# Building on-chip token lists: compares on VectorE unit by unit instead of in blocks on GpSimd

## The chip, the cores and the metric

The kernel runs on one core of one Trainium2 chip. The core has five engines that run their own instruction streams in order and wait for one another through semaphores: TensorE (PE in the profile; its weight loads are PEld), VectorE (DVE), ScalarE (ACT), GpSimd (POOL) and SyncE (SP), which here only issues transfers. The metric is the device time of one execution in microseconds (us); lower is better.

## The reference, cut to what matters

The reference is a gated linear-attention layer followed by a two-level mixture of experts. Only the part that the change touches is the routing: for each of 3072 tokens a group and an expert are chosen by the largest logit, and the token is sent through that expert with a weight.

```python
g_idx = np.argmax(x @ w_group, axis=1)            # 4 groups; g_w = softmax value of the winner
e_idx = np.argmax(xg @ w_expert[g], axis=1)       # 4 experts in each group; e_w likewise
...
h = np.maximum(xg[mask_e] @ w1[g, e], 0.0)
ye = h @ w2[g, e]
out[tok_idx] = (g_w * e_w)[:, None] * ye
```

`x` is the output of the attention, B=4 batches, 8 heads, 768 steps, 40 values a head. On the chip each expert fetches its tokens by a list of row numbers, so a list of tokens (and of weights) for each of the 16 experts must be made before an expert starts.

## The kernel before, in words

**Attention.** The sequence is cut into NCH=6 chunks of 128 steps; a chunk of one batch is a *unit*, 24 units (u = 0 to 23, u = 4 * chunk + batch). `unit(u)` writes the code of one step of a software pipeline: loads for unit u+3, decays for u+2, scores of u, and the end (`norm`, `rows`, `turn`) of unit u-1. On TensorE one step is, in order, the scores (`sp`, line 192), the product with the carried state (`it`, L218), logits of an earlier unit (`lg`, L333), the state update (`st`, L238), the values (`av`, L266) and the transposes of the finished rows (`tp`, L314). VectorE has, among others, the masked scores (`pt`, L198), the sum of carried and new part (`num`, L275), the denominators (`den`, L284 to L293), the finished rows (`x`, L301) and the state addition (`Cflat`, L256). GpSimd has four instructions in each step: the causal mask (`ab`, L154, for unit u+2), the weighted keys (`kw`, L205, for u+1), the decay of the state (`Cflat`, L245, for u) and the output gate times the inverse denominator (`sr`, L295, for u-1). VectorE's `x` needs `sr`; GpSimd's decay needs TensorE's `it`.

**Routing.** When the four logits of a chunk are there, `logits` starts a generator `route(c, ...)`, a *chore*. `go_on()` stands at five places of a step and advances the first chore by one stage (up to the next `yield`), so that routing is woven into the attention. The stages find the winners (`oh`), count ranks by small matmuls (L373 to L382), and give each token a slot number (`slots`, L405), from which `lo` (slot modulo 128) and `d` (the rest) follow. The chunk's share of the lists is a matmul: for each unit b of the chunk, `marks` (L424: a 128x128 0/1 table, an iota compared with `lo`), `eh` (L428: 128x48, a constant compared with `d`) and `put` (L433: `eh` times three columns of `vals`, 128x144 for a unit, two units in one instruction); then four matmuls (L443, written to the PSUM bank named `lg`) and an addition into `lists` (L446, L448). Which engine makes them is set by `q`: GpSimd for chunks 0 to 3 and for the first three units of chunk 4, VectorE for the last unit of chunk 4 and for chunk 5.

**Order.** Steps 2 to 21 (`MANUAL` = 22) are issued exactly as written. From step 22 on a scheduler orders the instructions. After chunk 2 is routed, the chore `first_experts` picks the first two experts and the loads of their weights follow on SyncE's queue, one piece (`w1s` or `w2s`) a step (`early_loads`, from step 15 in the order before). The first expert runs on the tokens of chunks 0 to 4 (fetch `xe`, L582); a second pass adds those of chunk 5.

The change and the prediction touch `route` (L406 to L448), the end of `unit` (L850 to L860), the loop over the steps (L964 to L969), and no code of the experts. The engine is picked by one line before:

```python
q = nc.gpsimd if c < NCH - 2 or (c < NCH - 1 and n > 1) else nc.vector
```

Of the kernel before, what the change touches and what calls it, by code (L numbers as in the profile page):

```python
# [57 lines left out]
def lstm_moe(ctx: ExitStack, tc: tile.TileContext, gates, qkT, nat, og, wcat, w1, w2, cst, tab, out):  # L58
# [281 lines left out]
    def route(c, b0, b1, bank):  # L340
# [74 lines left out]
        nc.vector.tensor_copy(lo, loi)
# [3 lines left out]
        q.tensor_tensor(d, slf, lo, op=ALU.subtract)
        marks = post.tile([P, n, P], F32R, name="marks", bufs=1)  # L420
        for b in range(n):
            if b == 2:
                yield
            q.tensor_scalar(marks[:, b], iota, lo[:, b:b + 1], None, op0=ALU.is_equal)  # L424
        yield
        eh = post.tile([P, n, NEH], F32, name="eh", bufs=1)
        for b in range(n):
            q.tensor_scalar(eh[:, b], ehc, d[:, b:b + 1], None, op0=ALU.is_equal)  # L428
        put = post.tile([P, n, 3, NEH], F32R, name="put", bufs=1)
        for b in range(0, n, 2):  # L430
            yield
            m = min(2, n - b)
            rt["last"] = q.tensor_tensor(put[:, b:b + m], bc(eh[:, b:b + m].unsqueeze(2), (P, m, 3, NEH)),  # L433
                            bc(vals.bitcast(F32)[:, us][:, b:b + m].unsqueeze(3), (P, m, 3, NEH)), op=ALU.mult)
        yield
# [4 lines left out]
        yield  # L440
        lp = rt["bank"][:, B * 36 + NE:B * 36 + NE + NLIST]
        for b in range(n):
            mm(lp, marks[:, b, :], put[:, b].rearrange("p i k -> p (i k)"), start=(b == 0), stop=(b == n - 1))  # L443
        yield
        if c + b0:
            nc.vector.tensor_tensor(lists, lists, lp, op=ALU.add)  # L446
        else:
            nc.vector.tensor_copy(lists, lp)  # L448
# [713 lines left out]
```

## Time and profile before

| what | value |
|---|---|
| three runs | 469.69, 473.66, 473.73 us (median 473.66) |
| the profiled execution, own time | 474.44 us |
| its span from the first to the last instruction | 472.9 us |
| busy in the span | TensorE 425.8, VectorE 332.8, ScalarE 268.5, GpSimd 195.9 us |
| mean granted TensorE clock | 0.955 of full speed |
| step 4 starts its scores | 42.13 us |
| steps 8, 12, 16, 20 | 67.60, 98.59, 135.08, 163.37 us |
| steps 21, 22 | 174.40, 179.95 us |
| first matmul of the first expert | 206.15 us |
| experts from there to the end | 266.8 us (472.9 - 206.15) |

Rows of the trace begin with start and length in us, then the engine, the line, the operation and its operands (result <- inputs); x4 is the number of instructions merged into the row (TensorE rows count a float32 matmul's two passes, so eight matmuls stand as x16). What stands in square brackets is the time for which the engine sat idle before it and the instruction it waited for. A row of stretches gives the stretch, its length, the busy time and number of instructions of each engine, the granted TensorE clock, the busy share of the transfer engines and their rate in GB/s.

### The profile page before, as it was taken

To read this page: it belongs to the slowest core of one execution; us is meant where nothing else is said; L and a number is where in the kernel's file an instruction comes from. 1 tells how busy PE (TensorE), PEld (TensorE's weight loads), DVE (VectorE), ACT (ScalarE), POOL (GpSimd) and SP (SyncE) were. 2 spreads that over 40 slices of the span, in tenths; PEclk is the share of its full clock that TensorE was granted. 3 is DMA by queue.
4 is the path that set the end of the run, shared out by engine and by line. 5 is a ranking of instruction groups with operands and counts; after the bars stand their busy time and mean duration, and the time that the engine had idled before them with its cause. 6 is when DMAs were issued, how large, how long until landed. Compare 5 with 4: busy or idle time off the path is not lost.

```text
span 472.9 us, 9535 instructions
## 1 busy us (share of the span) xinstructions
PE 425.8 (90%) x3421; PEld 404.4 (86%) x3421; DVE 332.8 (70%) x864; ACT 268.5 (57%) x619; POOL 195.9 (41%) x233
## 2 busy tenths in 40 slices
PE   7689997989799878989999999999999999898890
PEld 5579997878698778779999999999999999797890
DVE  7545777957577757779884765867676787988850
ACT  5556756473467662172764555665657655786640
POOL 7435465592835554106524134233322553232110
PEclk9797998998899989799999999999999999999996
DMA  4997674966559950254995366486557766353000
GB/s 149 292 300 232 224 249 129 338 182 227 150 177 309 322 196 18 67 195 154 381 372 201 123 214 230 161 303 203 215 188 278 256 236 226 102 208 138 14 16 9
DMA packets 24627, 94.40 MB, mean 200 GB/s; under 512 B 3888, under 2 KB 8072, under 8 KB 20994
## 3 DMA queue, kind: packets, MB, share of 16 engines
q1 hardware_dynamic: 20178, 77.95, 48.8%
q0 software_dynamic: 4128, 15.46, 8.8%
q8 instruction: 28, 0.46, 0.4%
q10 hardware_dynamic: 272, 0.36, 0.3%
q14 instruction: 21, 0.17, 0.1%
HBM read 84.21 MB, written 10.40 MB: 200 GB/s over the span
## 4 chain that ended last, share of the span: by engine, by line
PE 59%; DVE 15%; POOL 7%; DMA 5%; issue 5%; ACT 5%; SPq 1%; POOLq 0%; ACTq 0%; DVEq 0%
PE psh L741 17%; PE sp L192 6%; PE av L266 6%; PE po L762 5%; PE po L764 5%; PE po L763 5%; PE lg L333 3%; DMA ab<-a_d 3%; DVE w2l L640 2%; PE it L218 2%; PE tpm L675 2%; POOL marks L424 2%; DVE hh L698 2%; PE po L768 1%; DVE w1l L640 1%
## 5 line engine op out<-in xcount | busy, mean ns | idle before, releaser
L586 POOL DMA_INDIRECT out_dram<-y,li x35 | 49.8, 1422 | 147.2 <-ACT y L775 107.7
L762 PE MATMUL po<-w2h,hh 128*128 128x320 f32 (+1 forms) x208 | 65.8, 316 | 0.0
L763 PE MATMUL po<-w2l,hh 128*128 128x320 f32 (+1 forms) x208 | 64.2, 309 | 0.0
L764 PE MATMUL po<-w2h,hh 128*128 128x320 f32 (+1 forms) x208 | 64.1, 308 | 0.0
L182 ACT ACTIVATE ab<-ab,bcol 128x128 f32<-128x128 f32 x184 | 56.3, 389 | 13.0 <-POOL ab L154 12.4
L640 DVE TENSOR_TENSOR w2l<-w2s,w2h 128x640 fp32r<-128x640 f32 x64 | 49.8, 817 | 16.9 <-ACT w2h L638 16.7
L741 PE MATMUL psh<-xhl,w1h 128*128 128x256 f32 (+4 forms) x352 | 58.9, 288 | 1.2 <-DVE xhl L681 1.2
L192 PE MATMUL sp<-qk 128*128 128x128 f32 x384 | 53.0, 294 | 4.8 <-DMA qk<-in_qkT_dram 4.7
L266 PE MATMUL av<-nt,pt 128*128 128x128 f32 x384 | 56.2, 305 | 0.9 <-DVE pt L198 0.9
L192 PEld LDWEIGHTS sp<-qk 128*128 128x128 f32 x384 | 49.6, 208 | 5.7 <-issue 3.3
L266 PEld LDWEIGHTS av<-nt,pt 128*128 128x128 f32 x384 | 51.2, 214 | 2.3 <-DVE pt L198 1.3
L741 PEld LDWEIGHTS psh<-xhl,w1h 128*128 128x128 f32 x352 | 49.8, 189 | 1.9 <-DVE xhl L681 1.7
L582 POOL DMA_INDIRECT xg<-x_d,li x33 | 36.9, 1119 | 30.1 <-DVE cntr L564 18.5
L640 DVE TENSOR_TENSOR w1l<-w1s,w1h 128x1024 fp32r<-128x1024 f32 x32 | 39.0, 1220 | 12.2 <-ACT w1h L638 12.2
L638 ACT CAST w2h<-w2s 128x640 fp32r<-128x640 f32 x64 | 42.9, 727 | 1.1 <-DMA w2s<-in_w_dram 1.0
L154 POOL TENSOR_SCALAR_AFFINE_SELECT ab<-ab 128x1024 f32<-128x1024 f32 (+1 forms) x25 | 26.7, 1068 | 36.4 <-DMA ab<-a_d 32.5
L695 ACT ACTIVATE hh<-psh 128x512 fp32r<-128x512 f32 (+4 forms) x56 | 28.3, 506 | 21.0 <-PE psh L741 20.7
L698 DVE SCALAR_TENSOR_TENSOR hh<-psh,hh 128x256 fp32r<-128x256 f32 (+2 forms) x84 | 33.4, 429 | 9.0 <-ACT hh L695 8.6
L762 PEld LDWEIGHTS po<-w2h,hh 128*128 128x128 f32 (+1 forms) x208 | 38.8, 187 | 0.7 <-ACT hh L695 0.2
L764 PEld LDWEIGHTS po<-w2h,hh 128*128 128x128 f32 (+1 forms) x208 | 38.8, 187 | 0.1
L763 PEld LDWEIGHTS po<-w2l,hh 128*128 128x128 f32 (+1 forms) x208 | 38.9, 187 | 0.0
L198 DVE TENSOR_TENSOR pt<-sp,ab 128x512 f32<-128x512 f32 x48 | 32.8, 685 | 8.1 <-PE sp L192 7.1
(196 smaller groups left out, 957.4 us busy)
## 6 DMA issues: line engine op xcount, KB each, us to landing
w1s<-in_w_dram SPq DMA_DIRECT2D x12, 1536.0 KB
w2s<-in_w_dram SPq DMA_DIRECT2D x12, 1280.0 KB
ab<-a_d SPq DMA_DIRECT2D x23, 512.0 KB
nt<-in_nat_dram SPq DMA_DIRECT2D x24, 324.0 KB
qk<-in_qkT_dram SPq DMA_DIRECT2D x48, 160.0 KB
x_d<-x SPq DMA_DIRECT2D x24, 192.0 KB
sig<-in_og_dram SPq DMA_DIRECT2D x6, 640.0 KB
w1s<-in_w_dram SPq DMA_DIRECT2D x4, 768.0 KB
```

The source lines that it names most:

```text
L182: rt["exp"] = nc.scalar.activation(ab[:, j, :], ab[:, j, :], AF.Exp, bias=bcol[:, c, b * H + j:b * H + j + 1])
L192: mm(sp[:, jj, :], qk[:, j % 2, j // 2, :], qk[:, 2, j // 2, :], start=True, stop=True)
L266: mm(av[:, o:o + P], t["pm"][j // 4][:, j % 4, :], nt[:, o:o + P], start=True, stop=True)
L582: return nc.gpsimd.indirect_dma_start(out=o, out_offset=None, in_=src, in_offset=bass.IndirectOffsetOnAxis(ap=idx, axis=0))
L586: return nc.gpsimd.indirect_dma_start(out=out, out_offset=bass.IndirectOffsetOnAxis(ap=idx, axis=0), in_=y, in_offset=None, bounds_check=N ...
L638: nc.scalar.copy(a, src[:, s])
L640: lows.append(lambda: nc.vector.tensor_tensor(o[rows], src[rows, s], a[rows].bitcast(F32), op=ALU.subtract))
L698: rt["dve"] = nc.vector.scalar_tensor_tensor(hh[:, f:f + per, dst], src[:, :, t], 0.0, hr.bitcast(F32)[:, :, t], op0=ALU.max, op1=ALU.subt ...
L741: ins = mm(ps[:, g * W:(g + 1) * W], w[:, s], x, start=(n == 0), stop=(n == len(todo) - 1))
L762: mm(po[0:m], hh[:, f, t], w2h[:, s], start=st0, stop=False)
L763: mm(po[0:m], hh[:, f, t], w2l[:, s], start=False, stop=False)
L764: ins = mm(po[0:m], hh[:, f, tl], w2h[:, s], start=False, stop=sp0)
```

## The change

The compares (`marks`, `eh`) of all chunks go to VectorE, and for chunks 0 to 3 they are no longer made in one block inside the chore. Each unit's pair of compares with its product `put` becomes one task in a list `heavy`; the four matmuls (`placed`) and the addition (`summed`) are two more tasks. `unit` runs one task (two from step 18 on) behind `rows`, `state2` and `values` of the step, ahead of `turn`. At step 21 what is left in the list is run at the end. GpSimd keeps only the multiplications: `d`, the weights and `put`, the latter one unit at a time. For chunks 4 and 5 (`now`) everything stays in the chore, on VectorE, with one `put` for all units, so the three units of chunk 4 move from GpSimd to VectorE too. The chore has fewer stages.

```diff
-    chores = []
+    chores, heavy = [], []
...
-        q = nc.gpsimd if c < NCH - 2 or (c < NCH - 1 and n > 1) else nc.vector
+        now = c >= NCH - 2
+        q = nc.vector if now else nc.gpsimd
+        d = post.tile([P, n], F32, name="d")
+        q.tensor_tensor(d, slf, lo, op=ALU.subtract)
...
-        for b in range(n):
-            if b == 2:
-                yield
-            q.tensor_scalar(marks[:, b], iota, lo[:, b:b + 1], None, op0=ALU.is_equal)
-        yield
-        eh = post.tile([P, n, NEH], F32, name="eh", bufs=1)
-        for b in range(n):
-            q.tensor_scalar(eh[:, b], ehc, d[:, b:b + 1], None, op0=ALU.is_equal)
-        put = post.tile([P, n, 3, NEH], F32R, name="put", bufs=1)
-        for b in range(0, n, 2):
+        def mark(b, m):
...
+            for i in range(b, b + m):
+                nc.vector.tensor_scalar(t["marks"][:, i], iota, lo[:, i:i + 1], None, op0=ALU.is_equal)
+                nc.vector.tensor_scalar(t["eh"][:, i], ehc, d[:, i:i + 1], None, op0=ALU.is_equal)
+            rt["last"] = q.tensor_tensor(t["put"][:, b:b + m].rearrange("p b (i k) -> p b i k", i=3),
...
+        def placed():
+            lp = t["lp"] = rt["bank"][:, B * 36 + NE:B * 36 + NE + NLIST]
+            for b in range(n):
+                mm(lp, t["marks"][:, b], t["put"][:, b], start=(b == 0), stop=(b == n - 1))
+
+        def summed():
+            if c + b0:
+                nc.vector.tensor_tensor(lists, lists, t["lp"], op=ALU.add)
...
+        if now:
             yield
+            mark(0, n)
+            yield
+        else:
+            heavy.extend([lambda b=b: mark(b, 1) for b in range(n)] + [placed, summed])
+            yield
...
         go_on()
+        if heavy and u < MANUAL:
+            for _ in range(2 if u > 17 else 1):
+                task = heavy.pop(0) if heavy else None
+                if task:
+                    task()
         if not late(u - 1):
             run(turn, u - 1)
...
+            if u == MANUAL - 1:
+                do(heavy)
             do(early_loads, 1 if 14 <= u < 20 else 0)
```

**Place 1: GpSimd around step 8.** Before, after the `sr` of step 7 (names as above; the first column is the code line):

```order
L295 TENSOR_TENSOR sr<-sig,den 128x320
L419 TENSOR_TENSOR d<-slots,lo 128x4
L424 TENSOR_SCALAR marks<-ks,lo 128x128 x4
L428 TENSOR_SCALAR eh<-ks,d 128x48 x4
L154 AFFINE_SELECT ab<-ab 128x1024
L433 TENSOR_TENSOR put<-eh,vals 128x288
L205 TENSOR_TENSOR kw<-nt,ab 128x320
L245 TENSOR_TENSOR Cflat<-Cflat,dec 128x328
L433 TENSOR_TENSOR put<-eh,vals 128x288
```

Now, on the same engine from the small products of step 7 on:

```order
L415 TENSOR_TENSOR d<-slots,lo 128x4
L417 TENSOR_TENSOR wf<-sm,se 128x4
L418 TENSOR_TENSOR vals<-sm,se 128x4
L419 TENSOR_TENSOR vals<-wf,vals 128x4
L295 TENSOR_TENSOR sr<-sig,den 128x320
L430 TENSOR_TENSOR put<-eh,vals 128x144
L154 AFFINE_SELECT ab<-ab 128x1024
L205 TENSOR_TENSOR kw<-nt,ab 128x320
```

Eight compares have left GpSimd; one `put` for one unit stands directly behind `sr` and ahead of the mask, in steps 7 to 10 alike. The pair of compares it waits for stands on VectorE behind `x` and the state additions:

```order
L301 TENSOR_TENSOR x<-num,sr 128x320
L256 TENSOR_TENSOR Cflat<-Cflat,st 40x4x41 x2
L428 TENSOR_SCALAR marks<-ks,lo 128x128
L429 TENSOR_SCALAR eh<-ks,d 128x48
L275 TENSOR_TENSOR num<-num,av 128x328
```

**Place 2: TensorE, the list matmuls of chunk 0.** Before, in step 8, between state update and values:

```order
L333 MATMUL lg<-wc,xT 128x20 x3
L238 MATMUL st<-nt,kw 40x41 x8
L443 MATMUL lg<-put,marks 128x144 x4
L266 MATMUL av<-nt,pt 128x128 x8
L314 MATMUL tp<-cs,x 128x128 x2
```

Now, in step 11, behind the values:

```order
L333 MATMUL lg<-wc,xT 128x20 x3
L238 MATMUL st<-nt,kw 40x41 x8
L266 MATMUL av<-nt,pt 128x128 x8
L437 MATMUL lg<-put,marks 128x144 x4
L314 MATMUL tp<-cs,x 128x128 x2
```

They move three steps later, one step behind the last `put` they need. Those of chunk 1 move from step 12 to step 17, those of chunk 2 from step 14 to step 20, those of chunk 3 from step 20 into the scheduled part behind step 21, between pieces of unit 22.

**Place 3: SyncE, the first piece of expert weights.** Before, in the issue order (`w1s` is one half of a first weight matrix, `TENSOR_LOAD ewi` reads which expert it is):

```order
L308 DMA x_d<-x 128x384 x2
L161 DMA ab<-a_d 128x1024
L139 DMA qk_93<-in_qkT_dram 40x2x512
L140 DMA qk_93<-in_qkT_dram 40x1024
L170 DMA nt<-in_nat_dram 128x648
L308 DMA x_d<-x 128x384
L592 TENSOR_LOAD ewi x2
L600 ISA
L600 DMA w1s<-in_w_dram 128x1536
```

Now:

```order
L308 DMA x_d<-x 128x384 x2
L604 TENSOR_LOAD ewi x2
L612 ISA
L612 DMA w1s<-in_w_dram 128x1536
L161 DMA ab<-a_d 128x1024
L139 DMA qk_93<-in_qkT_dram 40x2x512
L140 DMA qk_93<-in_qkT_dram 40x1024
L170 DMA nt<-in_nat_dram 128x648
L308 DMA x_d<-x 128x384
```

The first piece is issued one step earlier (at the end of step 14), and six pieces instead of five stand between the loads of the attention; the sixth stood behind the last row store before.

More of the change, by code (lines that the diff above doesn't have):

```diff
@@ L408, in route @@
         nc.vector.tensor_scalar(loi, loi, P - 1, None, op0=ALU.bitwise_and)
+        lo = post.tile([P, n], F32, name="lo")
+        nc.vector.tensor_copy(lo, loi)
         yield
-        q = nc.gpsimd if c < NCH - 2 or (c < NCH - 1 and n > 1) else nc.vector
+        now = c >= NCH - 2
+        q = nc.vector if now else nc.gpsimd
+        d = post.tile([P, n], F32, name="d")
+        q.tensor_tensor(d, slf, lo, op=ALU.subtract)
         wf = post.tile([P, n], F32, name="wf")
@@ L425, in route @@
-        yield
-        eh = post.tile([P, n, NEH], F32, name="eh", bufs=1)
-        for b in range(n):
-            q.tensor_scalar(eh[:, b], ehc, d[:, b:b + 1], None, op0=ALU.is_equal)
-        put = post.tile([P, n, 3, NEH], F32R, name="put", bufs=1)
-        for b in range(0, n, 2):
-            yield
-            m = min(2, n - b)
-            rt["last"] = q.tensor_tensor(put[:, b:b + m], bc(eh[:, b:b + m].unsqueeze(2), (P, m, 3, NEH)),
-                            bc(vals.bitcast(F32)[:, us][:, b:b + m].unsqueeze(3), (P, m, 3, NEH)), op=ALU.mult)
@@ L435, in route @@
-        yield
+        t = {}
+        def mark(b, m):
+            if not t:
+                for a, w, dt in (("marks", P, F32R), ("eh", NEH, F32), ("put", NLIST, F32R)):
+                    t[a] = post.tile([P, n, w], dt, name=a, bufs=1)
+            sh = (P, m, 3, NEH)
+            for i in range(b, b + m):
+                nc.vector.tensor_scalar(t["marks"][:, i], iota, lo[:, i:i + 1], None, op0=ALU.is_equal)
+                nc.vector.tensor_scalar(t["eh"][:, i], ehc, d[:, i:i + 1], None, op0=ALU.is_equal)
+            rt["last"] = q.tensor_tensor(t["put"][:, b:b + m].rearrange("p b (i k) -> p b i k", i=3),
+                                         bc(t["eh"][:, b:b + m].unsqueeze(2), sh),
+                                         bc(vals.bitcast(F32)[:, us][:, b:b + m].unsqueeze(3), sh), op=ALU.mult)
@@ new lines, in placed @@
+        def placed():
[6 more added lines that the diff above has]
+            else:
+                nc.vector.tensor_copy(lists, t["lp"])
+        if now:
+            yield
+            mark(0, n)
+            yield
+        else:
+            heavy.extend([lambda b=b: mark(b, 1) for b in range(n)] + [placed, summed])
+            yield
@@ L439, in route @@
         nc.vector.tensor_tensor(nxt, cur, ohs, op=ALU.add)
[L440 to L448, printed above, removed]
+        if now:
+            yield
+            placed()
+            yield
+            summed()
     def go_on(n=1):
```

5 lines of the change are left out of this document (removed).

## The prediction

> **What bounds the kernel now.** The change works in the attention, so I read first how long its steps take. The stretches below are cut at the score starts of steps 4, 8, 12, 16, 20, 21, 22 and at the first expert matmul.
>
> ```profile
> 42.13:67.60 25.47, 25.11 (x273) 24.25 (x272) 19.09 (x58) 17.22 (x52) 13.01 (x20) 1.00 0.70 226
> 67.60:98.59 30.99, 27.85 (x277) 26.28 (x276) 26.08 (x61) 17.54 (x52) 19.00 (x31) 0.94 0.71 226
> 98.59:135.08 36.49, 30.03 (x281) 28.58 (x280) 24.09 (x75) 17.54 (x52) 23.07 (x39) 0.91 0.57 172
> 135.08:163.37 28.29, 25.72 (x273) 24.51 (x272) 20.65 (x62) 20.35 (x54) 13.66 (x21) 1.00 0.92 300
> 163.37:174.40 11.03, 7.97 (x56) 7.66 (x54) 6.05 (x15) 7.05 (x14) 8.75 (x12) 0.85 0.75 268
> 174.40:179.95 5.55, 5.55 (x52) 5.48 (x52) 4.09 (x16) 4.27 (x13) 0.00 (x0) 0.99 0.01 1
> 174.40:206.15 31.75, 27.35 (x194) 24.06 (x193) 22.44 (x104) 10.06 (x31) 7.38 (x14) 0.89 0.21 69
> ```
>
> Steps 4 to 7 make no list: TensorE is busy for 25.11 of 25.47 us at full clock, and is the bound. The next four steps take 5.52 us more with four more matmuls, the four after them 11.02 more with eight; the clock falls to 0.94 and 0.91. GpSimd's busy time rises from 13.01 to 19.00 and 23.07. Steps 16 to 19 lose only 2.82, at full clock but with transfers at 0.92. So the excess sits where lists are made. The waits say which one:
>
> ```profile
> PE lg L443 <- POOL put L433: 10.2, 8, 2.9
> PE tp L314 <- DVE x L301: 6.0, 5, 2.0
> DVE x L301 <- POOL sr L295: 22.5, 13, 3.2
> ```
>
> TensorE waits 10.2 us for `put` from GpSimd, and 6.0 for `x`, which itself waits for GpSimd's `sr`. In step 8, in order of time on TensorE, GpSimd and VectorE:
>
> ```profile
> 72.37 0.44 PE L443 MATMUL lg<-put,marks 128*128 128x144 f32 x2 [0.81 <-POOL put L433]
> 74.38 0.45 PE L443 MATMUL lg<-put,marks 128*128 128x144 f32 x2 [1.57 <-POOL put L433]
> 74.67 2.87 PE L266 MATMUL av<-nt,pt 128*128 128x128 f32 x16
> 82.58 2.05 PE L266 MATMUL av<-nt,pt 128*128 128x128 f32 x16
> ```
> ```profile
> 66.51 2.63 POOL L424 TENSOR_SCALAR marks<-ks,lo 128x128 fp32r<-128x128 f32 x4
> 69.13 1.51 POOL L428 TENSOR_SCALAR eh<-ks,d 128x48 f32<-128x48 f32 x4
> 70.59 1.08 POOL L154 TENSOR_SCALAR_AFFINE_SELECT ab<-ab 128x1024 f32<-128x1024 f32 x1
> 71.65 0.66 POOL L433 TENSOR_TENSOR put<-eh,vals 128x288 fp32r<-128x288 f32 x1
> 76.03 0.72 POOL L205 TENSOR_TENSOR kw<-nt,ab 128x320 f32<-128x320 f32 x1
> ```
> ```profile
> 70.62 6.17 DVE L439 TENSOR_TENSOR ohsum<-ohsum,ohs 128x16 bf16<-128x16 bf16 x1
> ```
>
> Eight compares hold GpSimd for 4.1 us. `put` is late, TensorE stands 0.81 and 1.57 us, and the values behind it take 2.87 instead of 2.05 us, since the clock was lowered in the pause. VectorE pays too: a 16-element addition that starts at 70.62 ends at 76.79, when GpSimd's unbroken run (66.51 to 76.75) is over.
>
> **The change part by part.** Of the 16 pairs that move out of GpSimd's blocks and the three of chunk 4, VectorE's price is in the trace, where it makes those of chunk 5:
>
> ```profile
> 209.06 0.28 DVE L424 TENSOR_SCALAR marks<-ks,lo 128x128 fp32r<-128x128 f32 x1
> 209.25 0.25 DVE L428 TENSOR_SCALAR eh<-ks,d 128x48 f32<-128x48 f32 x1
> 209.41 0.48 DVE L424 TENSOR_SCALAR marks<-ks,lo 128x128 fp32r<-128x128 f32 x2
> ```
>
> Starts lie 0.19 and 0.16 us apart, so a pair costs 0.35 us. What hides it: VectorE is busy 19.09 of 25.47 us in steps 4 to 7, 1.6 us idle a step; and in the pair's own place, here step 16:
>
> ```profile
> 139.42 0.49 DVE L301 TENSOR_TENSOR x<-num,sr 128x320 f32<-128x320 f32 x1 [1.00 <-POOL sr L295]
> 139.83 0.65 DVE L256 TENSOR_TENSOR Cflat<-Cflat,st 40x164 f32<-40x164 f32 x2
> 141.06 0.49 DVE L275 TENSOR_TENSOR num<-num,av 128x328 f32<-128x328 f32 x1 [0.58 <-PE av L266]
> ```
>
> the pair falls into the 0.58 us before `num`. Without that cover it would be 16 x 0.35 = 5.6 us. On GpSimd a `put` for one unit takes 0.43 us (below, x10, the minimum, which is the one 128x144 instruction). It stands behind `sr` and waits for its pair: 0.4 (`x`) + 0.6 (states) + 0.2 + 0.25 us, so with itself some 1.9 us from `sr` to the mask. Behind it in the queue stand `ab`, `kw` and the decay; their cover is GpSimd's wait for `it`, 24.6 us in 11 cases, 2.2 us each:
>
> ```profile
> L433 POOL TENSOR_TENSOR put<-eh,vals x10: 430/667/674, 71.7 to 187.1; 128x288 fp32r<-128x288 f32 x9, 128x144 fp32r<-128x144 f32 x1
> POOL Cflat L245 <- PE it L218: 24.6, 11, 4.8
> ```
>
> It just fits. This also empties GpSimd while VectorE runs the pair, so that the kind of collision seen at 70.62 doesn't arise there. The Trainium skill (SBUF — State Buffer, Who interferes with whom) has it that a VectorE instruction in a two-port mode, as an SBUF-to-SBUF compare with a scalar is, and a GpSimd instruction shut each other out for the whole instruction; the 6.17 us agree as far as a two-input addition shows it. By that rule the move is unwise if the pairs met GpSimd's mask and keys (1.8 us) each time; the sum would then be the 461 of the third rival.
>
> Now the stretches. Two list matmuls at full clock shift the next start by 0.28 us, so four cost 0.6 us; in the slow clock of step 14 (126.65 to 127.78, below) 1.1:
>
> ```profile
> 210.66 0.45 PE L443 MATMUL lg<-put,marks 128*128 128x144 f32 x2
> 210.94 0.56 PE L741 MATMUL psh<-xhl,w1h 128*128 128x256 f32 x3
> ```
>
> *Steps 8 to 11*, excess 5.52: the block and its waits are gone. The four matmuls of chunk 0 come in step 11 (0.6), a `put` made a step earlier; 0.2 for pairs where routing fills VectorE. Gain 4.7; bounds 3.5 and 5.5.
>
> *Steps 12 to 15*, excess 11.02: the blocks of chunks 1 and 2.
>
> ```profile
> 116.42 0.19 PE L373 MATMUL lg<-oh,lt_b 128*128 128x64 bf16 x1 [1.06 <-DVE oh L368]
> 124.79 0.52 PE L314 MATMUL tp<-cs,x 128*128 128x128 f32 x3 [2.01 <-DVE x L301]
> 126.65 1.33 PE L443 MATMUL lg<-put,marks 128*128 128x144 f32 x4 [0.66 <-POOL put L433]
> 127.78 3.15 PE L192 MATMUL sp<-qk 128*128 128x128 f32 x16
> ```
> ```profile
> 122.24 1.19 POOL L424 TENSOR_SCALAR marks<-ks,lo 128x128 fp32r<-128x128 f32 x2
> ```
>
> The rank matmuls' wait of 1.06 is VectorE's burst of routing and stays. The 2.01 goes mostly: the `sr` that this `x` waited for stood behind two compares of 1.19 us together and, further ahead, two more. No list is placed in these steps. I leave 2.5 (1.06, 0.5 for `x`, the rest for the earlier weights): gain 8.5; bounds 5 and 10.
>
> *Steps 16 to 19*, excess 2.82, from transfers:
>
> ```profile
> 149.91 1.09 POOL L154 TENSOR_SCALAR_AFFINE_SELECT ab<-ab 128x1024 f32<-128x1024 f32 x1 [3.14 <-DMA ab<-a_d]
> 159.29 1.09 POOL L154 TENSOR_SCALAR_AFFINE_SELECT ab<-ab 128x1024 f32<-128x1024 f32 x1 [6.20 <-DMA ab<-a_d]
> ```
> ```profile
> w1s<-in_w_dram SPq DMA_DIRECT2D x4, 768.0 KB
> ```
>
> The mask waits for `ab`, and `sr` behind it. Weights come a step earlier and six pieces instead of five lie among the loads; a `w1s` half (768 KB) at the 300 GB/s of this stretch is 2.6 us. Steps also come faster than before, so this grows. Plus 0.6 for chunk 1's matmuls. Loss 2.0; bounds 0 and 6 (twice the excess now).
>
> *Step 20*, 11.03 against 5.55 in step 21 (the row of GpSimd and the last one are of the stretch behind it):
>
> ```profile
> 182.18 0.20 POOL L419 TENSOR_TENSOR d<-slots,lo 128x3 f32<-128x3 f32 x1 [9.19 <-DVE lo L415]
> ```
> ```profile
> 169.77 0.45 PE L443 MATMUL lg<-put,marks 128*128 128x144 f32 x2 [2.87 <-POOL put L433]
> 187.19 0.72 PE L443 MATMUL lg<-put,marks 128*128 128x144 f32 x3 [1.79 <-POOL put L433]
> ```
>
> Chunk 3's block and its 2.87 go; chunk 2's matmuls come (0.6), with their last `put` in the same step (0.7 of waiting). Gain 4.2; bounds 2 and 5.
>
> *Steps 21 to the first expert*: for chunk 4 GpSimd needs 182.18 to 187.19, 5.0 us; VectorE three pairs (1.05), small products and one `put` of about 0.6, some 2.2. The difference, 2.8, covers the 1.79 of TensorE's wait and the slower matmuls behind it. Against it stand chunk 3's matmuls, 0.6, and three or four of its pairs, 1.05 us, ahead of chunk 4's on VectorE, half of it exposed. Gain 1.7; bounds -2 and 4.
>
> The experts are unchanged and shift as a whole; the row stores, gathers and the weights' last pieces come no later. Sum: -4.7 - 8.5 + 2.0 - 4.2 - 1.7 = -17.1 us. Against the profiled execution's own 474.44 us this gives **457 us**; that execution lies 0.8 us above the median of the three runs (473.66), less than they differ among themselves, so I leave it.
>
> **The rivals.** *Transfers take it back.* The attention's bytes are the same, in less time. For it: 0.92 busy in steps 16 to 19, waits of 3.14 and 6.20. Against: 0.57 in steps 12 to 15 and next to nothing after step 20. Then steps 14 to 19 run at the pace of the loads, the loss there is its bound of 6 and step 15 gives back 2 to 4: 457 + 4 + 3 = 464 us.
>
> *The waits only move.* GpSimd's small products and `put` still hang on routing, VectorE (26.08 of 30.99 busy in steps 8 to 11) becomes the one TensorE waits for. For it: the 1.06 for `oh`, the 6.0 for `x`. Against: VectorE's own time there holds 6.17 us of standing. If half of the gains of steps 8 to 15 and all of the last stretch fail: 457 + 6.6 + 1.7 + 4 (step 20) = 469, up to 473 us; that is also the case in which the change does nothing to be measured.
>
> *Shutting out.* The pairs wait for running masks and keys after all: 16 x 1.8 = 29 us on VectorE against 1.6 us of slack a step: some 4 us come through, 461 us. For it: the 6.17; against: GpSimd stands at `put` meanwhile.
>
> *Slower: the `put` in GpSimd's order.* Each of the 16 waits for VectorE's pair, with the mask, keys, decay, `sr` and so `x` and TensorE's transposes queued behind. Its price is 1.9 us a step, 31 us in all if nothing hides it: 488. It decides from 17.1 / 16 = 1.07 us exposed a step. For it: GpSimd's queue has only 2.2 us of slack and the routing steps less. Against: the mask and keys are for one and two units ahead.
>
> **How the numbers follow.** Chances: forecast 0.58 (own range 451 to 462), transfers 0.18, shutting out 0.07, waits only move 0.10, slower 0.07. 450 to 468 holds all but the last two and the best corner. A measurement of this kernel can tell about 1%, 4.7 us, from no change. Faster by more (below 469): 0.58 + 0.18 + 0.07 = 0.83 and a little of the waits that move, 0.84; within 1%: 0.09; slower: 0.07.
>
> **What would show it.** Right: no wait of TensorE for `put` above some 0.7 us; no slow values (2.87) behind the list; no VectorE addition of 16 elements above 1.1 us; the step 8 to 12 stretch near 26.3 us at clock 1.00, 12 to 16 near 28; GpSimd busy some 20 us less (four blocks of 4.1 and chunk 4's three pairs), VectorE 19 x 0.35 = 6.7 us more and its 6.17 of standing less. Steps 16 to 19 about 30 us, the mask waiting for `ab` in more of them. Experts still about 267 us. Wrong: compares on VectorE far above 0.28 us, GpSimd's decay starting late for `put`, or TensorE's waits for `x` above 6 us in total.

## The result, and the profile after

The changed kernel takes 460.86 us, median of six executions (456.16 to 463.0), against 473.7 us (469.69 to 475.12, six executions) for the kernel before on the same chip: a ratio of 0.9725, 95% interval 0.967 to 0.978. A second series of six (run 9 below) gave 460.74 us and 0.9802 (0.9732 to 0.9873), which alone leaves open whether the gain is over 2%. Ratios compare only executions within 1.5% of the fastest of their kernel, medians take all of them; in the second series that leaves four of eleven of the kernel before, so its ratio is nearer to 1 than that of the medians (460.74 to 474.19 us). The forecast was 457 us, its range 450 to 468.

The stretches are cut as in the prediction, at the score starts of steps 8, 12, 16, 20 and 21 and at the first expert matmul. First the changed kernel:

```profile
63.62:90.15 26.53, 25.82 (x277) 24.83 (x276) 22.33 (x69) 17.12 (x52) 16.06 (x25) 1.00 0.79 263
90.15:118.62 28.47, 25.64 (x274) 24.54 (x272) 22.91 (x81) 17.11 (x52) 13.96 (x23) 1.00 0.70 220
118.62:147.94 29.32, 27.51 (x277) 26.48 (x276) 23.20 (x67) 20.34 (x54) 14.72 (x22) 0.94 0.96 335
147.94:156.88 8.94, 6.55 (x55) 6.18 (x54) 8.71 (x26) 7.20 (x15) 5.24 (x6) 1.00 0.84 270
156.88:190.09 33.21, 30.89 (x198) 26.57 (x196) 25.53 (x116) 10.15 (x31) 4.36 (x7) 0.78 0.24 78
190.09:459.60 269.51, 252.19 (x1826) 244.52 (x1826) 191.64 (x440) 156.87 (x300) 89.45 (x72) 0.97 0.51 185
```

Its second profile:

```profile
65.05:91.58 26.53, 25.81 (x277) 24.82 (x276) 22.33 (x69) 17.12 (x52) 15.53 (x25) 1.00 0.80 261
91.58:121.64 30.06, 27.22 (x274) 26.11 (x272) 22.83 (x81) 17.12 (x52) 14.22 (x23) 0.94 0.70 226
121.64:148.49 26.85, 26.01 (x278) 24.89 (x276) 22.03 (x66) 20.28 (x54) 15.25 (x22) 1.00 0.95 331
148.49:157.93 9.44, 7.92 (x55) 7.47 (x54) 8.40 (x27) 7.20 (x15) 5.65 (x6) 0.83 0.86 303
157.93:190.74 32.81, 30.21 (x197) 25.66 (x197) 25.05 (x115) 10.15 (x31) 4.06 (x7) 0.81 0.24 79
```

And the kernel before, a second time, cut in the same way:

```profile
67.31:98.24 30.93, 27.92 (x278) 26.35 (x277) 25.83 (x61) 17.53 (x52) 18.98 (x31) 0.94 0.74 226
98.24:134.68 36.44, 30.01 (x281) 28.60 (x280) 24.10 (x75) 17.54 (x52) 23.02 (x39) 0.91 0.57 173
134.68:162.74 28.06, 25.68 (x274) 24.52 (x273) 20.62 (x62) 20.34 (x54) 13.66 (x21) 1.00 0.92 303
162.74:173.53 10.79, 7.74 (x55) 7.43 (x54) 6.04 (x15) 7.05 (x14) 8.73 (x12) 0.87 0.78 271
173.53:205.50 31.97, 27.57 (x194) 24.20 (x193) 22.46 (x104) 10.05 (x31) 7.37 (x14) 0.88 0.21 67
```

Side by side, in us (first and second profile of each kernel; the last column is the difference of the means, worked out from these):

| stretch | before | after | predicted | measured |
|---|---|---|---|---|
| to step 8 | 67.60, 67.31 | 63.62, 65.05 | 0 | -3.1 |
| steps 8 to 11 | 30.99, 30.93 | 26.53, 26.53 | -4.7 | -4.4 |
| steps 12 to 15 | 36.49, 36.44 | 28.47, 30.06 | -8.5 | -7.2 |
| steps 16 to 19 | 28.29, 28.06 | 29.32, 26.85 | +2.0 | -0.1 |
| step 20 | 11.03, 10.79 | 8.94, 9.44 | -4.2 | -1.7 |
| step 21 to the first expert | 31.75, 31.97 | 33.21, 32.81 | -1.7 | +1.1 |
| experts | 266.75, 269.3 | 269.51, 270.16 | 0 | +1.8 |
| span | 472.9, 474.8 | 459.6, 460.9 | -17.1 | -13.6 |

Most of the gain, 11.6 of 13.6 us, sits in steps 8 to 15, where the lists were made in blocks. From step 20 on the prediction asked for 5.9 us, and the mean gives back 1.2 (-1.7 + 1.1 + 1.8 = +1.2). The waits of the changed kernel (who <- for whom: us in total, times, longest):

```profile
PE lg L437 <- POOL put L430: 1.3, 2, 1.1
PE tp L314 <- DVE x L301: 0.9, 1, 0.9
```
```profile
POOL put L430 <- DVE eh L429: 20.6, 11, 2.6
DVE x L301 <- POOL sr L295: 13.3, 12, 2.9
POOL Cflat L245 <- PE it L218: 11.2, 10, 2.7
```

TensorE's two were 10.2 and 6.0 us before, VectorE's for `sr` 22.5; the one wait for `x` that is left stands ahead of step 8. GpSimd's wait for `it`, 24.6 before, was to cover the new `put`: it is 13.4 us shorter, and GpSimd now waits 20.6 us for comparisons. VectorE's 16-element addition that took 6.17 us takes 0.69 us at most. VectorE makes a comparison for `marks` in 0.279 us (median of 24), as predicted; GpSimd is busy for 177.7 us instead of 195.9 (the second profiles: 178.2 and 196.0), VectorE for 338.8 and 336.2 instead of 332.8 and 335.5.

### The profile page after: what moved, and what is told of

The parts are those of the page before. It is cut to its first block, busy times and chain, and to the rows that moved or that the text cites. A ratio compares the mean times of both kernels' runs of the same rounds, so it can differ in the third digit from the quotient of the medians.

```text
span 459.6 us, 9540 instructions
## 1 busy us (share of the span) xinstructions
PE 423.6 (92%) x3421; PEld 402.3 (88%) x3421; DVE 338.8 (74%) x906; ACT 267.7 (58%) x619; POOL 177.7 (39%) x197
## 4 chain that ended last, share of the span: by engine, by line
PE 65%; DVE 18%; issue 4%; ACT 4%; DMA 3%; POOL 3%; SPq 1%; POOLq 0%; ACTq 0%
PE psh L753 20%; PE sp L192 7%; PE po L774 5%; PE av L266 5%; PE po L775 5%; PE po L776 5%; PE lg L333 4%; PE it L218 3%; DVE w2l L652 3%; PE tpm L687 2%; DVE w1l L652 2%; DMA a_d<-A__119 2%; PE po L780 2%; DVE pt L198 1%; PE busy L121 1%
## 5 line engine op out<-in xcount | busy, mean ns | idle before, releaser
L182 ACT ACTIVATE ab<-ab,bcol 128x128 f32<-128x128 f32 x184 | 56.3, 388 | 10.3 <-POOL ab L154 9.8
L753 PE MATMUL psh<-xhl,w1h 128*128 128x256 f32 (+4 forms) x352 | 60.1, 293 | 0.2 <-DVE xhl L693 0.2
L266 PE MATMUL av<-nt,pt 128*128 128x128 f32 x384 | 53.5, 292 | 3.1 <-DVE pt L198 2.4
L192 PE MATMUL sp<-qk 128*128 128x128 f32 x384 | 49.0, 281 | 4.4 <-DMA qk<-in_qkT_dram 4.4
L753 PEld LDWEIGHTS psh<-xhl,w1h 128*128 128x128 f32 x352 | 51.0, 194 | 1.3 <-DVE xhl L693 1.1
L266 PEld LDWEIGHTS av<-nt,pt 128*128 128x128 f32 x384 | 47.7, 200 | 4.7 <-DVE pt L198 2.8
L192 PEld LDWEIGHTS sp<-qk 128*128 128x128 f32 x384 | 45.6, 194 | 5.0 <-DMA qk<-in_qkT_dram 2.9
```

Of the source, the lines that this page charges most:

```text
L182: rt["exp"] = nc.scalar.activation(ab[:, j, :], ab[:, j, :], AF.Exp, bias=bcol[:, c, b * H + j:b * H + j + 1])
L192: mm(sp[:, jj, :], qk[:, j % 2, j // 2, :], qk[:, 2, j // 2, :], start=True, stop=True)
L266: mm(av[:, o:o + P], t["pm"][j // 4][:, j % 4, :], nt[:, o:o + P], start=True, stop=True)
L753: ins = mm(ps[:, g * W:(g + 1) * W], w[:, s], x, start=(n == 0), stop=(n == len(todo) - 1))
```

## The experiments

The times to the next start are read in the same cuts. "Gather" below is the first fetch of rows (`xe`) on GpSimd, which needs the first expert's finished list.

**1. The other engine alone.** The kernel before, with only the comparisons of chunks 0 to 3 on VectorE, in their old blocks.

```diff
-            q.tensor_scalar(marks[:, b], iota, lo[:, b:b + 1], None, op0=ALU.is_equal)
+            (nc.vector if c < NCH - 2 else q).tensor_scalar(marks[:, b], iota, lo[:, b:b + 1], None, op0=ALU.is_equal)
...
-            q.tensor_scalar(eh[:, b], ehc, d[:, b:b + 1], None, op0=ALU.is_equal)
+            (nc.vector if c < NCH - 2 else q).tensor_scalar(eh[:, b], ehc, d[:, b:b + 1], None, op0=ALU.is_equal)
```

> The kernel before, with one part of the change alone: the comparisons for marks and eh of chunks 0 to 3 go to VectorE, still four units in one block at their old places; the products (put) stay on GpSimd, two units at a time. Theory A, it was GpSimd's uninterrupted block of about 4.1 us in its fixed order (four marks at 0.63-0.72 us, four eh at 0.43-0.45) that came once in four steps: the block shrinks to two products of 0.67 us, so most of the gain is there, steps 8 to 15 take 55-59 us (before 67.5, after 55.0) and the whole 461-465 us. Rival B, the spreading over the steps is what pays, and a block on VectorE (four times 0.27 + 0.24 = 2.0 us) holds TensorE as the one on GpSimd did: steps 8 to 15 at 62-67 us, the whole 468-473 us.

Measured: 459.34 us, ratio 0.9659 (0.9606 to 0.9712). Steps 8 to 11, steps 12 to 15, and from step 21's scores to the gather:

```profile
63.97:90.70 26.73, 26.17 (x277) 24.96 (x276) 23.23 (x69) 17.33 (x52) 15.11 (x23) 1.00 0.80 260
90.70:121.77 31.07, 26.79 (x282) 25.53 (x280) 27.37 (x88) 17.22 (x52) 15.84 (x24) 1.00 0.67 204
158.52:178.74 20.22, 17.73 (x140) 16.62 (x138) 15.38 (x79) 6.34 (x21) 5.33 (x14) 0.92 0.06 22
```

57.8 us in steps 8 to 15 (26.73 + 31.07): theory A holds there, rival B falls; the whole is 1.7 us below A's range. The block on VectorE costs something only in steps 12 to 15, where VectorE is busy 27.37 of 31.07 us.

**2. The spreading alone.** The changed kernel, with those comparisons back on GpSimd, one unit a step.

```diff
-                nc.vector.tensor_scalar(t["marks"][:, i], iota, lo[:, i:i + 1], None, op0=ALU.is_equal)
-                nc.vector.tensor_scalar(t["eh"][:, i], ehc, d[:, i:i + 1], None, op0=ALU.is_equal)
+                q.tensor_scalar(t["marks"][:, i], iota, lo[:, i:i + 1], None, op0=ALU.is_equal)
+                q.tensor_scalar(t["eh"][:, i], ehc, d[:, i:i + 1], None, op0=ALU.is_equal)
```

> The changed kernel, with the comparisons of chunks 0 to 3 put back on GpSimd, but one unit a step as the change places them (0.72 + 0.45 + 0.43 = 1.6 us a step on GpSimd in place of 0.43). Theory A, the block in one place was the cost and not GpSimd's sum of work: GpSimd has 3.4 us of other work in a step of 6.6 us, so 1.2 us more fit in, steps 8 to 15 take 55-58 us and the whole 460-464 us. Rival B', GpSimd's busy time itself is the bound or shuts VectorE out: about 19 us come back on GpSimd, of which a half shows: steps 8 to 15 at 61-66 us, the whole 467-472 us.

Measured: 457.52 us, 0.962 (0.9555 to 0.9684). Steps 8 to 11, 12 to 15, step 20, and step 21 to the first expert and to the gather:

```profile
63.23:89.62 26.39, 25.99 (x277) 24.88 (x276) 19.42 (x60) 17.10 (x52) 19.00 (x31) 1.00 0.79 260
89.62:119.32 29.70, 27.21 (x274) 26.16 (x273) 22.29 (x76) 17.12 (x52) 18.41 (x30) 0.94 0.73 231
146.59:154.57 7.98, 6.58 (x55) 6.18 (x54) 6.81 (x21) 7.09 (x15) 7.16 (x10) 1.00 0.93 322
154.57:186.08 31.51, 29.86 (x198) 25.68 (x196) 23.66 (x107) 9.71 (x30) 9.40 (x15) 0.80 0.28 94
154.57:176.50 21.93, 20.58 (x166) 19.60 (x164) 20.02 (x93) 6.75 (x21) 7.21 (x14) 0.93 0.11 39
```

In steps 8 to 11 GpSimd is busy for 19.00 us, exactly as in the kernel before (19.00), and VectorE has no comparison to make; yet the stretch takes 26.39 instead of 30.99 us at full clock. So neither GpSimd's sum of work nor the engine was the cost, but the unbroken block in one place of its order, ahead of list matmuls that TensorE had next. Either half of the change removes it. This run also keeps the later place of the list matmuls; whether cutting the block up would do with the matmuls in their old place was not tried. The three other profiles with the comparisons spread on GpSimd (runs 7 and 8) have 26.2 to 27.8 us in steps 8 to 11. The whole is again below A's range (460 to 464). The comparisons take longer on GpSimd here (`marks` 0.597 to 0.981 us, median 0.888) and are hidden all the same.

**3. Chunk 4 back on GpSimd.**

```diff
-        q = nc.vector if now else nc.gpsimd
+        q = nc.gpsimd if c < NCH - 2 or (c < NCH - 1 and n > 1) else nc.vector
+        v = nc.vector if c < NCH - 2 else q
...
-                nc.vector.tensor_scalar(t["marks"][:, i], iota, lo[:, i:i + 1], None, op0=ALU.is_equal)
-                nc.vector.tensor_scalar(t["eh"][:, i], ehc, d[:, i:i + 1], None, op0=ALU.is_equal)
+                v.tensor_scalar(t["marks"][:, i], iota, lo[:, i:i + 1], None, op0=ALU.is_equal)
+                v.tensor_scalar(t["eh"][:, i], ehc, d[:, i:i + 1], None, op0=ALU.is_equal)
```

> The changed kernel, with all of chunk 4's three units (comparisons, product and the small products) put back on GpSimd, where they were before the change. Theory C, VectorE became the bound of the tail when it took chunk 4's three pairs and their product beside chunk 3's three pairs and the splits: the stretch from step 21 to the first expert matmul falls from 33.2 us by 1 to 3 us, and the first expert with it; the whole 457-460 us. Rival D, the tail's loss is only the lower TensorE clock of that window and not VectorE: the stretch stays at 32-34 us, the whole 460-462 us. Rival E, GpSimd is later in the tail than VectorE is: the stretch grows by 1 to 3 us, the whole 462-465 us.

Measured: 464.64 us, 0.9745 (0.9697 to 0.9793); the stretch from step 21 to the first expert is 37.29 us, 4.1 longer (in a profile of the slowest of its four executions). On TensorE:

```profile
174.58 0.70 PE L438 MATMUL lg<-put,marks 128*128 128x144 f32 x2 [4.21 <-POOL put L431]
```

Rival E, and past its size: TensorE stands 4.21 us for GpSimd's `put`. For chunk 4 the move to VectorE is right, as the prediction had it. Theory C fails with this edit, but not its idea, as runs 5 and 8 show.

**4. The weights a step later.**

```diff
-            do(early_loads, 1 if 14 <= u < 20 else 0)
+            do(early_loads, 1 if 15 <= u < 20 else 0)
```

> The changed kernel, with the expert's early weight pieces issued from step 15 on in place of step 14 (five in place of six in the steps, the sixth behind them). Theory F, the transfers are what steps 16 to 19 wait for (DMA share 0.96 there, 1.03 us longer than before): the piece fewer gives back 0.5 to 1.5 us in steps 15 to 19 and costs up to 0.5 us at the first expert: the whole 459.5-461 us. Rival G, it is a shift only: the same bytes come later, steps 16 to 19 are unchanged and the first expert's weights are late: the whole 461-463 us.

Measured: 460.69 us, 0.9687 (0.9629 to 0.9745). Steps 16 to 19, and step 21 to the first expert:

```profile
119.76:148.45 28.69, 26.03 (x277) 24.88 (x276) 22.39 (x66) 20.35 (x54) 14.75 (x22) 1.00 0.92 300
157.59:190.54 32.95, 30.50 (x198) 25.90 (x196) 26.06 (x116) 10.15 (x31) 4.89 (x7) 0.80 0.28 92
```

The whole lies in F's range, but the stretch it rests on, 28.69 us, lies between the two profiles of the changed kernel (29.32 and 26.85), and G's later first expert isn't there either: no effect that these runs can tell.

**5. Each pair twice.**

```diff
-                nc.vector.tensor_scalar(t["marks"][:, i], iota, lo[:, i:i + 1], None, op0=ALU.is_equal)
-                nc.vector.tensor_scalar(t["eh"][:, i], ehc, d[:, i:i + 1], None, op0=ALU.is_equal)
+                for _ in range(1 if now else 2):
+                    nc.vector.tensor_scalar(t["marks"][:, i], iota, lo[:, i:i + 1], None, op0=ALU.is_equal)
+                for _ in range(1 if now else 2):
+                    nc.vector.tensor_scalar(t["eh"][:, i], ehc, d[:, i:i + 1], None, op0=ALU.is_equal)
```

> The changed kernel, with each of the sixteen pairs of comparisons of chunks 0 to 3 made twice on VectorE (0.27 + 0.24 us more a step, 8.2 us in all; the result is the same). Theory K, a pair has cover: VectorE waits for GpSimd's masks and rows in each step of 8 to 15, so the second pair goes into that wait: steps 8 to 15 at 55-57.5 us, the whole 460.5-464 us. Rival L, VectorE is now the next bound in these steps: most of the 0.51 us comes out per step, steps 8 to 15 at 58-60 us, the whole 465-469 us.

Measured: 471.33 us (467.08 to 474.64, ten executions), 0.9945 (0.9906 to 0.9984). The profile is of the fastest of the ten. Steps 8 to 11, 12 to 15, step 20, and step 21 to the gather:

```profile
64.05:91.55 27.50, 25.86 (x277) 24.84 (x276) 24.52 (x77) 17.32 (x52) 15.62 (x25) 1.00 0.80 249
91.55:120.71 29.16, 25.71 (x273) 24.56 (x272) 23.79 (x83) 17.11 (x52) 13.85 (x22) 1.00 0.67 209
149.55:160.25 10.70, 6.55 (x56) 6.19 (x54) 9.81 (x33) 7.20 (x15) 5.24 (x6) 1.00 0.74 248
160.25:186.78 26.53, 21.88 (x171) 20.06 (x169) 24.02 (x112) 7.49 (x24) 2.92 (x5) 0.90 0.07 24
```

Steps 8 to 15 are in K's range (56.66 us), but the second pair has cover only in part: at the same clock of 1.00 the two stretches are 0.97 and 0.69 us longer than in the first profile of the changed kernel, for 2.19 and 0.88 us more work on VectorE. The time of the whole lands beyond L; more of it comes out in step 20 (+1.5 us against the mean 9.2) and behind it: the gather stands 26.5 us behind step 21's scores instead of 22.9 and 22.3. That is where VectorE sets the pace. Why the median is another 4 us above the profiled execution stays open; the other nine executions have mean granted clocks of 0.945 to 0.957 against its 0.966.

**6. Fillers in the tail.** TensorE's clock was at half for 20 us there; three matmuls of ones fill the wait that came ahead of it.

```diff
+        if not rt["manual"]:
+            with tc.issue_after(rt["rk"].ins):
+                busy(3)
         yield
```

> The changed kernel, with three 512-column filler matmuls behind the rank matmuls of the last two parts (chunks 4 and 5), where TensorE waits 0.68 us for masked keys in the last scheduled steps. Theory M, the tail's missing gain is the granted TensorE clock: it fell to half behind a window of 3.41 us in which TensorE worked only 1.87 us, and stayed down for 20.5 us through transposes and small matmuls into the first expert; with the window filled the clock stays up, the stretch from step 21 to the first expert goes from 33.2 to 28-31 us, the experts from 269.5 to 267-268.5 us, and the whole to 455-459 us. Rival N, the engines and not the clock set the tail's time: the fillers only take TensorE time, 0 to +0.7 us, the whole 460.5-462 us. Rival O, the fall comes anyway in another window: within 1 us of the changed kernel, with a low stretch of over 6 us still in the tail.

Measured: 458.2 us, 0.9648 (0.961 to 0.9686). Step 21 to the first expert, and to the gather:

```profile
155.80:187.54 31.74, 29.82 (x201) 24.71 (x199) 24.96 (x115) 10.15 (x31) 4.99 (x7) 0.84 0.26 85
155.80:177.97 22.17, 20.47 (x168) 18.59 (x167) 20.45 (x98) 6.51 (x20) 2.81 (x5) 0.99 0.08 26
```

The whole is in M's range and the half-clock stretch is 10.2 us instead of 20.5, but the stretch itself gained only 1.1 to 1.5 us, less than M's 2 to 5, and the experts nothing (269.66 us). Two more runs took it apart.

**7. Spread on GpSimd, with more fillers, twice.** The edit of run 2, that of run 6, and

```diff
-                busy(2)
+                busy(4)
```

behind the transposes of the last three units.

> The comparisons of chunks 0 to 3 on GpSimd, one unit a step (as in the run that only spread them), with the same three fillers behind the rank matmuls of chunks 4 and 5 and four fillers in place of two behind the transposes of the last three units. Theory M: the run that only spread had its clock at half for 13.7 us of the tail, worth up to 6.8 us less what other waits would take; kept up, the stretch from step 21 to the first expert goes from 31.5 to 27-29.5 us and the whole to 452-456 us. Rival N: the six more fillers of 0.22 us come out on top: the stretch at 32-33 us, the whole 458-459.5 us.

> The fastest version so far once more (comparisons of chunks 0 to 3 on GpSimd, one unit a step, and fillers in the tail), for its time beside the kernel before and for a second profile of the tail. Theory X, the fillers keep the clock up but the first expert can't start before its gathered rows are there: the gather stands 21-22 us behind step 21's scores as without fillers, TensorE waits for the rows (xe), and the stretch to the first expert is 30.5-32.5 us with the clock above 0.9; the whole 455-458 us. Rival M, the clock was the limit: the stretch is below 30 us and the whole below 455 us. Rival R, the earlier median was luck of a few executions: the whole 459-462 us like the changed kernel's.

Measured: 456.48 us, 0.9571 (0.9517 to 0.9625), then 459.18 us, 0.9673 (0.9625 to 0.9721). The first whole lies between the ranges of M and N; the stretch in its profile is 32.4 us, N's and not M's. In the second run's profile, step 21 to the first expert, to the gather, and the wait of TensorE ahead of that expert:

```profile
156.23:186.82 30.59, 26.30 (x207) 22.71 (x206) 23.73 (x107) 9.81 (x30) 9.16 (x15) 0.99 0.28 96
156.23:177.86 21.63, 21.00 (x177) 19.27 (x176) 20.07 (x93) 7.04 (x23) 6.99 (x14) 1.00 0.11 40
```
```profile
185.11 0.44 PE L690 MATMUL tpm<-cs,xe 128*128 128x128 f32 x2 [3.23 <-DMA xe<-x_d,li]
```

The chain of work that ended last, from the gather on (start, length, engine, result, line):

```profile
177.86 1.22 POOL xe L597
179.37 5.70 DMA xe<-x_d,li
185.11 0.56 PE tpm L690 x3
```

The clock is up (0.99) and the stretch is only 0.9 us shorter than in run 2 (31.51, clock 0.80): TensorE gets through sooner and then waits 3.23 us for the fetched rows, 4.65 us in the first profile. M falls, X holds in the stretch: with the clock up, the first expert starts when the gathered rows have landed, and the gather is issued when VectorE has the list. X's range for the whole is missed; 459.18 us lies in R's, so the first median was in part a matter of few executions. The twelve together have their median at 459.0 us, against 460.9 for the twelve of the changed kernel; runs 2 and 6 lie at 457.5 and 458.2. All that is some 2 to 3 us below the change, but the intervals of the ratios overlap, with one another and with that of the change.

**8. The splits ahead of the tail,** on the changed kernel and on that of run 2.

```diff
-            do(early_splits, {16: 1, 17: 1, 18: 2, 20: 2, 21: 1}.get(u, 0))
+            do(early_splits, {16: 1, 17: 2, 18: 2, 19: 2}.get(u, 0))
```

> The changed kernel, with the first expert's last three weight splits (w2l, 0.82 us each on VectorE) made in steps 18 to 20 instead of behind step 21. Theory V, the tail is set by VectorE's work up to the first expert's list: VectorE is busy 21.0 of the 22.9 us from step 21's scores to the first gather in the changed kernel, 15.1 of 19.7 us in the kernel before, and the first expert starts 10 us behind the gather in all runs. Three splits fewer there bring the gather 1.5-2.5 us forward (20.4-21.4 us behind step 21's scores) and the stretch to the first expert to 30.7-31.7 us from 33.2; the whole 458-460 us. Rival W, VectorE is as full in steps 18 to 20 (8.8 of 9 us in two stretches there), so all of it comes back ahead of step 21: the whole 460.5-462 us. Rival M, the clock sets the tail and not VectorE: the stretch changes by less than 1 us or with the low windows only.

> Both edits that helped or should: the comparisons of chunks 0 to 3 on GpSimd, one unit a step, and the last three weight splits of the first expert in steps 18 to 20. Theory V: VectorE loses 1.8 us of comparisons and 2.45 us of splits ahead of the first list against the changed kernel, the gather stands 19.5-20.5 us behind step 21's scores, the stretch to the first expert is 29-30.5 us, the whole 453.5-456.5 us. Rival W: steps 18 to 20 grow by what the tail gains, the whole 457-459 us.

Measured: 462.33 us, 0.9838 (0.9756 to 0.9921), and 460.52 us, 0.9785 (0.9719 to 0.9851); the changed kernel beside them had 0.9802. On the changed kernel, step 21 to the gather and to the first expert:

```profile
159.17:180.40 21.23, 20.17 (x171) 18.79 (x169) 20.39 (x102) 4.90 (x19) 2.77 (x5) 1.00 0.10 34
159.17:189.69 30.52, 28.45 (x198) 23.84 (x196) 23.87 (x115) 7.85 (x27) 4.90 (x7) 0.85 0.27 90
```

The tail did as V said, or a little better (21.23 and 30.52 us). The whole did as W said, or a little worse: nothing is gained. Where it came back can't be read off cleanly, since the clock was down for 6.8 us in steps 12 to 15 of this execution. The second kernel's profile is of the slowest of its six executions (465.45 us); its gather stands 21.5 us behind, not V's 19.5 to 20.5, and TensorE waits 3.47 us for the rows. Its whole is above the ranges of V and W. The two edits don't add up.

**9. Both kernels again.**

> The kernel before, unchanged, once more with a profile. Theory P, the 4 us that the changed kernel gained ahead of step 8 are the phase of the clock's windows and not the change: the stretch to step 8 then differs between executions of the kernel before, from 63 us (clock up throughout) to 68 us; steps 8 to 15 are 66-68.5 us whatever the phase. Rival Q, the change's order of loads or pools moves the start too: the stretch to step 8 is 67-68.5 us again.

> The changed kernel, unchanged, once more with a profile, beside the two others. What is the same in both profiles is the kernel's, what differs is the phase of the clock's windows: steps 8 to 11 at 26.5, 12 to 15 at 28-30, 16 to 19 at 26.5-29.5, the gather 22-23.5 us behind step 21's scores, the whole 459-462 us. The stretch to step 8 is 63-66 us; at 67-68 us, as twice in the kernel before, the 4 us there would not be the change's.

Their rows are in the first section. Steps 8 to 11 repeat within 0.06 us in each kernel; steps 12 to 15 and 16 to 19 of the changed kernel move by +1.6 and -2.5 us, each with a half-clock window that sits in the one stretch or the other; of the 2.5 at most 1.7 (half of 3.41) can be that window's. The stretch to step 8 was 67.3 us again in the kernel before, so P's spread didn't show. It is in Q's range, but Q's cause doesn't fit: run 1 has the loads and pools of the kernel before, and 63.97. In the other twelve profiles of this study it is 63.1 to 65.9.

## Why the prediction was right or wrong

**The whole: right, in part by luck.** The span moved by -13.6 us for -17.1. The stretches that the sum priced, from step 8 to the first expert, gained 12.3 us; the start, for which the sum had nothing, gave 3.1, and the experts took 1.8.

**The cause: right, and shown.** GpSimd's 4.1-us block in one place of its order held TensorE. Run 1 moves the comparisons to the other engine and leaves everything else in its place, run 2 cuts the block up on the same engine, and they bring steps 8 to 11 to 26.7 and 26.4 us.

**Steps 8 to 11: right,** -4.4 for -4.7. The accounting can be closed from the trace: the waits for `put` were 0.81 + 1.57 = 2.38 us, and the lowered clock behind them cost the rest. The window with the wait and the one behind it, in the kernel before:

```profile
72.16:75.57 3.41, 1.63 (x12) 1.49 (x13) 3.41 (x1) 2.71 (x10) 3.41 (x6) 1.00 0.35 105
75.57:78.98 3.41, 3.21 (x16) 2.91 (x16) 3.33 (x7) 0.58 (x3) 1.19 (x2) 0.50 0.08 28
```

A window of 3.41 us at half speed with TensorE busy for 3.21 is worth about 1.6 us, by estimate; 2.4 + 1.6 = 4.0 of the 4.4.

**Steps 12 to 15: right in kind,** -7.2 for -8.5. The 1.06 for `oh` stayed, as said. What was not foreseen: in one profile of two the clock is at half for a window behind the remaining waits, and the stretch is 1.6 us longer. Nine of the twelve profiles other than those of the kernel before have such a window there.

**Steps 16 to 19: the size failed,** -0.1 for +2.0. The mask's wait for `ab`, which was to grow ("Steps also come faster than before, so this grows"), fell there from 11.9 and 11.7 us to 4.1 and 4.7. The transfers are fuller (0.96 and 0.95 for 0.92), but moved 335 and 331 GB/s where "a `w1s` half (768 KB) at the 300 GB/s of this stretch is 2.6 us" held the rate of before for a limit. It was not one. That the piece's place matters is not shown (run 4).

**Step 20: half,** -1.7 for -4.2. TensorE's 2.87 for chunk 3's block went. The step that failed is "chunk 2's matmuls come (0.6), with their last `put` in the same step (0.7 of waiting)". In the first profile:

```profile
152.78 2.21 PE L266 MATMUL av<-nt,pt 128*128 128x128 f32 x16 [1.31 <-DVE pt L198]
156.36 0.34 PE L437 MATMUL lg<-put,marks 128*128 128x144 f32 x1 [1.08 <-POOL put L430]
```

1.08 for the `put`, and 1.31 for masked scores, of which the prediction had nothing: VectorE is busy 8.71 of the 8.94 us. The comparisons are part of what fills it: the step takes 7.9 to 8.0 us in the three profiles of runs 2 and 7, with them on GpSimd (VectorE busy for 6.8), 8.9 and 9.4 in those of the changed kernel, and 10.7 with each made twice (run 5). With them on GpSimd and the splits moved ahead (run 8), VectorE is full again and the step is 9.4.

**Step 21 to the first expert: the step that failed,** +1.1 for -1.7. It counted chunk 3's pairs at 1.05 us, "half of it exposed", and took TensorE's waits for what bounds the stretch. What bounds it first is the chain over VectorE. Before and after, from step 21's scores to the gather (VectorE is the third busy time):

```profile
174.40:194.11 19.71, 17.38 (x131) 16.65 (x131) 15.06 (x79) 6.03 (x19) 5.19 (x12) 0.85 0.04 15
```
```profile
156.88:179.78 22.90, 20.80 (x162) 19.67 (x160) 21.02 (x99) 6.51 (x20) 2.19 (x6) 0.90 0.06 21
```

Before, VectorE had 4.65 us to spare there; now 1.88. It makes eight pairs instead of one, and six of the masked scores instead of four. All versions that keep chunk 4 on VectorE stand at its busy time plus 0.7 to 2.9 us: 20.0 gives 21.9 (run 2), 20.4 gives 21.2 (run 8), 24.0 gives 26.5 (run 5). Behind the gather the first expert follows 9.0 to 10.7 us later, 9.0 at a clock of 0.99 (run 7) and 10.3 at half (190.09 - 179.78); before it was 12.0 (206.15 - 194.11).

In the changed kernel itself the chain that ended last does not go through the gather. It leaves VectorE at 173.5 us (178.3 in the second profile) and goes on over TensorE, at half clock from 175.28 (178.62); when TensorE reaches the expert's rows (`tpm`), it does not wait for them:

```profile
186.58 0.54 PE lg L333 x2
187.12 0.85 PE tpm L687 x3
```

So two paths of nearly the same length lie behind VectorE's work, TensorE's at half clock and the gather's. Against run 2, run 7 shortens TensorE's alone and its two profiles end 0.9 us later and 0.9 us sooner; run 8 takes splits off VectorE ahead of both, and the stretch of the changed kernel is 2.3 to 2.7 us shorter.

**Experts: +1.8 for 0, open.** In the first profile the clock came back only some 6 us behind the first expert matmul, worth about 3 us by estimate. But run 7's second profile, at half clock for only 2.8 us there, has 270.6 us, and the second profile of the kernel before 269.3, so the term is within what executions differ.

**The start: -3.1 for 0, not explained.** None of the changed instructions stands ahead of step 5, and run 1, with the code of before and other engines for the comparisons alone, has 63.97. What differs is the clock: ahead of step 8 it is at half for four and three windows of 3.41 us in the two profiles of the kernel before, and for none to two in the other twelve (63.1 and 63.2 us with none, 64.0 to 65.9 with two). At up to 1.7 us a window, by estimate, that is enough for the 3.1. In both profiles of the kernel before the last of these falls follows a wait of TensorE for `x` of 1.85 us at 32 us; but run 2 waits 2.90 us there and keeps its clock. What brings the falls, the kernel or the execution, stays open, and with it up to 3 us of the 13.

**The rivals.** "The waits only move" came true from step 20 on and nowhere else. "Transfers take it back", 464, is nearer to the result than the forecast (3.1 us against 3.9), for a wrong reason: steps 16 to 19 lose nothing. "Shutting out" is there, with another victim than the pairs. VectorE's denominator behind a pair, and GpSimd's mask, in the changed kernel:

```profile
64.69 1.08 DVE L284 SCALAR_TENSOR_TENSOR den<-num 128x8 f32<-128x8 f32 x1
```
```profile
64.65 1.09 POOL L154 TENSOR_SCALAR_AFFINE_SELECT ab<-ab 128x1024 f32<-128x1024 f32 x1
```

Its usual length is 0.17 us; it starts 0.04 behind the mask and ends with it. Seven of the 24 denominators take 0.4 to 1.08 us so, 4.9 us more in all (4.3 in the second profile); before, the longest took 0.51. Run 2, without the pairs on VectorE, has five, 2.9 us, so the pairs are not all of it. The section cited in the prediction (the Trainium skill, SBUF — State Buffer, Who interferes with whom) also says that a VectorE instruction with two SBUF inputs contends with a GpSimd instruction that reads SBUF; the denominator and the mask are such a pair, and the two rows agree. Four of the seven fell in steps 8 to 12, where VectorE had time, and two in step 20, where it had not. "The `put` in GpSimd's order" did not decide: GpSimd stands 20.6 us for comparisons, and TensorE 1.3 us for `put` in all.

## What to carry to other kernels

An engine that works in a fixed order and feeds others several times a step can be late by its longest unbroken run and not by its sum: cut that run up first, and moving the work to another engine may then be unnecessary (run 2 keeps GpSimd at its 19.00 us and is as fast). Work has cover only where the receiving engine waits for something in that very place; ask for each stretch which chain ends it, since the pairs cost next to nothing in steps 8 to 11 (26.53 us with them on VectorE, 26.39 without) and about 1 us in step 20 alone. And keeping the clock up buys little where a transfer behind another chain decides the next start: 0.9 us at most here.

## What the runs showed of the hardware

The granted clock moves on a grid. In the kernel before it falls at 17.55, 34.61, 75.57, 106.29, 126.77, 171.15 and 188.21 us; all gaps are whole multiples of 3.413 us, and the phase differs between executions. The Trainium skill (TensorE: Matmul & The Clock Gate, What's actually happening) states this free-running window of 3413 ns, and all fourteen profiles agree. Two things that its table of the two states says there they do not bear out. The clock falls without an idle window: 1.63 us of work in 3.41 was too little (row at 72.16 above), and so was 2.44 ahead of the fall at 141.15 in the changed kernel. And a window that the profile counts as busy need not release it. In the changed kernel, the window ahead of the fall and the six behind it:

```profile
171.87:175.28 3.41, 1.87 (x16) 1.43 (x17) 3.41 (x25) 0.77 (x3) 0.00 (x0) 1.00 0.16 58
175.28:195.76 20.48, 20.26 (x92) 16.82 (x91) 13.47 (x70) 7.99 (x17) 2.18 (x2) 0.50 0.32 103
```

TensorE is busy for 20.26 of 20.48 us and stays at half speed through values, 20-column logits, transposes and a few fillers, until a window full of expert matmuls. In the kernel before, at 171.15, one window was enough in which TensorE was busy throughout with values and transposes. Which work counts, these runs don't tell.
